# An attention, soft-MoE and MLP kernel: the first pair of heads in an order of its own, its stacks written in place

## The chip, the cores and the metric

The kernel runs on one core of one Trainium2 chip. The metric is device time in microseconds (us) of one execution. Engines are named as in the profile: PE is TensorE (PEld its weight loads), DVE is VectorE, ACT is ScalarE, POOL is GpSimd, SP is SyncE, whose queue issues nearly all DMAs.

## What is computed

Three layers follow one another, all in fp32.

```python
# attention: B = 4, H = 8, S = 576, D = 64
q_rot, k_rot = rotate(q), rotate(k)              # x1*cos - x2*sin, x1*sin + x2*cos
scores = q_rot @ k_rot.T / sqrt(D)
attn = exp(scores - max(scores)); attn /= sum(attn) + 1e-9
x = (attn @ v)                                   # heads side by side: 2304 rows of 512
# soft MoE: 8 experts, 4 slots each, hidden size 1024
logits = x @ phi
slot_in = softmax(logits, over rows).T @ x
slot_out[e] = relu(slot_in[e] @ w1[e]) @ w2[e]
x = softmax(logits, over slots) @ slot_out
# MLP, hidden size 2048
h = x @ w_in
out = (h * tanh(softplus(h))) @ w_out
```

## The kernel before

**Stages.** Attention takes the 32 heads in 16 pairs (0 to 325 us), the experts follow, and then the MLP (from 375 us to the end). While attention runs, other engines already convert the weights of the MLP into pairs of words and load expert weights into buffers that come free.

**Scores.** A head has 576 rows: 512 main rows, in four blocks of 128, and 64 rest rows. Both operands of the score product are split into a high and a low part (fp32r, a form of fp32 that PE takes faster). For each pair they lie in two *stacks*: `qk_st` holds the scaled q of both heads (columns QA and QAR for head 0, QB and QBR for head 1) and the k of both heads (from KC); `k2_st` holds k a second time with the halves exchanged. The high part lies on 64 of the 128 partitions and the low part on the other 64, so that one matmul against `qk_st` and one against `k2_st` make up the product (`s_mm`, L328 ff.). A score step takes 4 matmuls of 128x288, or 8 for the rest rows (`s_mm2`).

**One pair** goes through these steps, each a short name in the order table:
- `ropek`, `ropeq`, `ropeR`: rotation of k, q and the rest rows (`rotate`, L239: two products, a difference and a sum)
- `Hk`, `Hq`, `G`: four PE transposes of k or q (`m_k`, `m_q`), and one of the rest rows (`m_rem`)
- `hka`, `hqa`, `ga`: ACT writes the high part from PSUM into the tile `parth`; `hkd`, `hqd`, `gd`: DVE writes the low part into `partl`
- `dk`, `dq`: 8 and 4 DMAs from SBUF to SBUF that put the parts into the stacks (`stack_dma`, L320)
- S0 to S8: score steps, M0 to M8: row maxima on DVE (`nmax`), E0 to E8: exponentials on ACT (`P`); the even ones belong to head 0, the odd ones to head 1, 8 is the rest rows of both
- T0 to T7, K, R, Q: transposes of the exponentials, t0 to t7, k, ...: their copies from PSUM into `PT` (which engine copies is in `EVAC`, L38)
- A0 to A4 and B0 to B4: the product with v; X, x, Y, y, z, w: scaling of its output and its product with phi
- `ci`, `Ca`, `Cb`, `Cs`, `co`: load, scaling on ACT (`w<-w`), rounding on DVE, sum on POOL and store of a block of MLP weights; `turns` (L719) says which block falls to which pair
- `ld`: loads of q and k for a later pair, and of rest rows for a later batch

**Order.** The order of work on each engine is written out by hand. `PLAN` (L28) is the list of steps of one period, and "@1" after a step means that it is done for the pair before. The loop at the end of attention goes through the periods and records each step in turn. So an instruction that waits holds up all that stands behind it on its engine. All recorded instructions have one line, L83.

**The first pair** has no pair ahead of it that would build its stacks. The setup (L663 ff.) does it: DVE ropes k, the rest rows and q; PE transposes them; ACT and DVE write the parts; `stack_copy` on ACT and POOL moves them into the stacks (seven copies), and one `stack_dma` (two DMAs) moves the low part of head 1's k. In between, `busy` puts idle matmuls on PE. In period 0 the steps that feed pair 1 are moved to later places (`moved`, `shifted`).

**PSUM.** The score buffers `s` are two tiles of two banks (`ps_s`), and four tiles of one bank (`ps_m`) serve all else.

**Weights.** `fetch` (L131) loads a block of expert weights into a buffer of the rings. At `LAST_SCRATCH`, when the scratch of the conversions is free, three blocks are fetched one after the other.

Of the kernel before, what the change touches and what calls it, by code (L numbers as in the profile page):

```python
# [41 lines left out]
def kernel(  # L42
# [185 lines left out]
    def load_rem(b):  # L228
        t = work(1, 3, (H, D))
        dma(out=t[0:R], in_=q[b, :, 512:S, :].rearrange("h s d -> s h d"))  # L230
        dma(out=t[R:128], in_=k[b, :, 512:S, :].rearrange("h s d -> s h d"))
        rem_raw[b] = t
# [473 lines left out]
    main_hi(-1, "q")  # L706
    stack_copy(act.copy, "q", 0, "h")
    main_lo(-1, "q")
    stack_copy(pool_.tensor_copy, "q", 0, "l")
    stack_copy(act.copy, "q", 1, "h")  # L710
    stack_copy(act.copy, "q", 1, "l")
    load_v(1)
# [100 lines left out]
    moved = {(-1, n) for n in ("G", "ga", "gd", "Hk")}  # L813
    moved |= {(0, n) for n in ("hka", "hkd", "dk", "Hq", "hqa", "hqd", "dq", "ropek", "ropeq")}
    steps["ropeq1"] = lambda p: rope_pair(1, "q", dve, ws[1])
    moved |= {(-1, "ld")}
# [436 lines left out]
```

## Time and profile before

| | |
|---|---|
| time, median of 3 runs | 607.31 us (606.13 to 609.28) |
| profiled execution, own time | 609.64 us |
| profiled execution, span | 607.9 us |
| mean granted clock of PE | 0.997 |
| PE busy | 588.2 us, 97% of the span |
| DVE, ACT, POOL busy | 384.1, 341.5 and 213.9 us |
| DMA | 108.82 MB, mean 179 GB/s |

The runs are timed without a profile; the rows further down come from the one profiled execution, whose time is 2.33 us above the median. Its span is 1.74 us shorter than its time. A granted clock of 1.00 is 2.4 GHz, one of 0.50 is 1.2 GHz. Matmuls are pipelined, so that the durations of neighbours overlap.

### The profile page before, as it was taken

How to read it: one execution, taken by the hardware profiler on the slowest of the kernel's cores; microseconds unless marked ns; L12 is line 12 of the kernel's file. 1: busy time of each engine (PE TensorE's matmuls, PEld its weight loads, DVE VectorE, ACT ScalarE, POOL GpSimd, SP SyncE). 2: the span in 40 equal slices, each digit the busy share in tenths (PEclk: the TensorE clock that was granted, in tenths of full speed). 3: DMA queues.
4: the chain of work that ended last, by engine and by line, in shares of the span. 5: the costliest groups of instructions: out<-in, count | busy, mean ns of one | idle time of the engine just before them, and what ended most of it. 6: DMA issues, size and time to landing. Idle time of an engine off the chain costs nothing.

```text
span 607.9 us, 11291 instructions
## 1 busy us (share of the span) xinstructions
PE 588.2 (97%) x4110; PEld 467.0 (77%) x4110; DVE 384.1 (63%) x808; ACT 341.5 (56%) x778; POOL 213.9 (35%) x258
## 2 busy tenths in 40 slices
...
GB/s 173 233 260 213 208 229 267 252 230 263 262 254 260 256 255 275 228 167 312 245 214 379 196 380 402 173 88 156 11 20 85 0 1 1 66 38 0 2 1 105
DMA packets 59288, 108.82 MB, mean 179 GB/s; under 512 B 12768, under 2 KB 25184, under 8 KB 58720
## 3 DMA queue, kind: packets, MB, share of 16 engines
...
## 4 chain that ended last, share of the span: by engine, by line
PE 80%; DMA 6%; DVE 3%; ACT 2%; issue 1%; SPq 0%; ACTq 0%; DVEq 0%
PE o_ps L1137 32%; PE s L83 12%; PE m_av L83 10%; PE t L83 7%; DMA qk_st<-parth 4%; PE hp L1103 3%; PE h_ps L933 2%; PE so_ps L999 2%; PE m_lg L83 2%; PE warm L557 2%; DMA qk_st<-partl 1%; PE m_x L83 1%; PE m_q L83 1%; ACT P L83 1%; PE m_si L83 1%; PE tk L83 1%
## 5 line engine op out<-in xcount | busy, mean ns | idle before, releaser
L83 DVE TENSOR_REDUCE nmax<-s 128x1 f32<-128x576 f32 x144 | 106.8, 751 | 27.1 <-PE s L83 25.6
L83 ACT ACTIVATE P<-s,nmax 128x576 f32<-128x576 f32 x144 | 107.1, 744 | 18.3 <-DVE nmax L83 17.4
L1137 PE MATMUL o_ps<-wo_l,gh 128*128 128x512 f32 x288 | 112.9, 392 | 0.0
L1137 PE MATMUL o_ps<-wo_h,gh 128*128 128x512 f32 x288 | 112.9, 392 | 0.0
L83 PE MATMUL s<-qk_st 128*128 128x288 f32 x320 | 102.5, 337 | 5.3 <-ACT P L83 4.9
L1110 ACT ACTIVATE room<-hp 128x512 f32<-128x512 f32 x72 | 43.0, 599 | 106.6 <-PE hp L1103 102.0
L1137 PE MATMUL o_ps<-wo_h,gl 128*128 128x512 f32 x288 | 100.6, 390 | 1.0 <-DVE gl L1118 1.0
L83 PE MATMUL s<-k_st,qk_st 128*128 128x288 f32 x320 | 89.2, 295 | 0.0
L83 POOL TENSOR_TENSOR w<-w,cs 128x512 f32<-128x512 f32 (+2 forms) x74 | 86.5, 1190 | 0.9
L83 PE MATMUL t<-cs,P 128*128 128x128 f32 x576 | 83.9, 273 | 0.4 <-ACT P L83 0.4
L83 PEld LDWEIGHTS s<-qk_st 128*128 128x128 f32 x320 | 60.2, 188 | 21.5 <-ACT P L83 9.7
L83 POOL TENSOR_TENSOR w<-w 128x256 f32<-128x256 f32 (+2 forms) x86 | 65.7, 785 | 17.4 <-ACT P L83 14.8
L1112 DVE CAST gh<-room 128x512 fp32r<-128x512 f32 x49 | 20.9, 427 | 79.4 <-ACT room L1110 79.2
L83 PEld LDWEIGHTS t<-cs,P 128*128 128x128 f32 x576 | 68.2, 142 | 0.9 <-ACT P L83 0.7
L83 ACT COPY PT<-t 128x512 f32<-128x512 f32 (+1 forms) x112 | 61.3, 558 | 10.4 <-PE t L83 9.6
L1137 PEld LDWEIGHTS o_ps<-wo_h,gl 128*128 128x128 f32 x288 | 53.9, 188 | 13.3 <-DVE gl L1118 1.7
L1137 PEld LDWEIGHTS o_ps<-wo_h,gh 128*128 128x128 f32 x288 | 54.1, 188 | 9.3
L1137 PEld LDWEIGHTS o_ps<-wo_l,gh 128*128 128x128 f32 x288 | 54.3, 189 | 8.9 <-DVE wo_l L990 0.2
L83 PEld LDWEIGHTS s<-k_st,qk_st 128*128 128x128 f32 x320 | 60.6, 189 | 0.0
L1118 DVE TENSOR_TENSOR gl<-room,gh 128x512 fp32r<-128x512 f32 x72 | 49.6, 690 | 4.6
L83 PE MATMUL m_av<-PT,w 128*64 128x320 f32 (+1 forms) x384 | 52.0, 411 | 0.0
L83 POOL TENSOR_TENSOR c_all<-c_all,tmp 128x64 f32<-128x64 f32 (+1 forms) x44 | 20.9, 474 | 57.6 <-DVE tmp L83 55.8
...
## 6 DMA issues: line engine op xcount, KB each, us to landing
...
w<-in_moe_w_in_dram SPq DMA_DIRECT2D x16, 512.0 KB, 5.4
...
room<-in_moe_w_out_dram SPq DMA_DIRECT2D x12, 512.0 KB, 3.5
...
```

What stands on the lines that cost most here:

```text
L83: return lambda *a, **k: tc.keep_in_program_order(f(*a, **k))
L557: tc.keep_in_program_order(nc.tensor.matmul(ps, lhsT=ident, rhs=ident, start=True, stop=True))
L933: nc.tensor.matmul(h_ps[32 * g:32 * g + 32, fh, :], lhsT=si_t[:, c, 32 * e:32 * e + 32], rhs=parts[1, e, hf][0][:, cc * F1 + fh * 512:cc * ...
L999: nc.tensor.matmul(so_ps[32 * g:32 * g + 32, :], lhsT=h_t[eg][:, c, 32 * g:32 * g + 32], rhs=parts[2, e, hf][0][:, cc * DM:(cc + 1) * DM], ...
L1103: pin(nc.tensor.matmul(hp[:, x, :], lhsT=wst[:, f * 128:(f + 1) * 128], rhs=ct[:, i * 256:(i + 1) * 256], start=True, stop=True))
L1110: pin(nc.scalar.activation(out=gg, in_=hp, func=AF.Mish))
L1112: pin((nc.scalar.copy if 0 < u < NG * GR else nc.vector.tensor_copy)(gh, gg))
L1118: pin(nc.vector.tensor_tensor(out=gl, in0=gg, in1=gh.bitcast(F32), op=ALU.subtract))
L1137: pin(nc.tensor.matmul(ops[i, n], lhsT=g_[:, cols], rhs=w_[f], start=(j == 0 and (x, k) == (0, 0)), stop=(j == NG - 1 and all(y[0] != n fo ...
```

## The change

- **PSUM in pair 0.** There are three score buffers and two small ones at first. Two of the score buffers are `xk` and `xq`, which take the transposed k and q of pair 0. After `PLAN0` the pools are closed, and the old ones (two and four) are opened.
- **Setup.** The load of k is issued on ACT's queue, and ACT's table load after it. The rest rows of heads 0 and 1 are loaded alone, behind q; those of the other six heads come after the loads of pair 1. k and q are transposed once. ACT writes eleven high parts from PSUM straight into their places in the stacks, DVE eleven low parts. `parth`, `partl`, the seven copies and the two stack DMAs aren't used for pair 0. The first two score steps stand between the parts. There are 10 and 8 idle matmuls instead of 14, 9 and 12 in the setup, and none in pair 0.
- **POOL** now ropes q of pair 1 too, which DVE did (`ropeq1`).
- **Order of pair 0.** `PLAN0`, a list of its own, takes the place of `moved` and `shifted`. t1 and t3 of pair 0 are copied by DVE. The steps `G`, `ga`, `gd` and `Hk` that feed pair 2 come early in period 1 (`late_feed`). The loads `ld:1`, `ld:2` and the conversion load `ci1` stand at the end of `PLAN0`.
- **Conversions.** The first one moves from pair 0 to pair 1; there are 20 as before.
- **Weight fetch.** At `LAST_SCRATCH` two blocks are fetched instead of three; the third is fetched behind `dk` of pair 14, which holds the stack DMAs of pair 15's k.

The order of the instructions shows it on PE first, from the start of the program (`busy` is idle matmuls, `m_k`, `m_rem` and `m_q` are the transposes, `s` the scores). Before:

```order
L83 MATMUL busy<-c_all 128x128 x14
L83 MATMUL m_k<-cs,w_7_0_96 128x128 x4
L83 MATMUL m_rem<-cs,w_5_1_98 128x128
L83 MATMUL busy<-c_all 128x128 x9
L83 MATMUL m_q<-cs,w_7_0_96 128x128 x4
L83 MATMUL busy<-c_all 128x128 x12
L83 MATMUL s<-qk_st_119 128x288
L83 MATMUL s<-k_st_117,qk_st_119 128x288
```


With the change:

```order
L90 MATMUL busy<-c_all 128x128 x10
L90 MATMUL xk<-cs,w_0_0_85 128x128 x4
L90 MATMUL xk<-cs,w_5_1_98 128x64
L90 MATMUL xq<-cs,w_5_1_98 128x64
L90 MATMUL busy<-c_all 128x128 x8
L90 MATMUL xq<-cs,w_0_0_85 128x128 x4
L90 MATMUL s<-qk_st_119 128x288
L90 MATMUL s<-k_st_117,qk_st_119 128x288
```


The scores follow the transposes of q with no idle matmuls between, and the transposes go into `xk` and `xq`.

On ACT, in pair 0, from its first exponentials on (`P` is an exponential, `parth` a high part for pair 1, `PT` a copy out of PSUM, `w<-w` the scaling of weight words). Before:

```order
L83 ACTIVATE P,z_121<-s,nmax 128x576 x4
L83 CAST parth<-m_rem 128x2x2x64
L83 ACTIVATE parth<-m_k 128x512
L83 ACTIVATE w_4_0_93<-w_4_0_93 128x512 x2
L83 COPY PT<-t 128x4x128 x2
L83 ACTIVATE P,z_121<-s,nmax 128x576
L83 COPY PT<-t 128x4x128
L83 ACTIVATE parth<-m_q 128x512
L83 ACTIVATE P,z_121<-s,nmax 128x576
L83 COPY PT<-t 128x4x128
L83 COPY PT<-tk 128x256
L83 COPY PT<-t 128x4x128
```


With the change:

```order
L90 ACTIVATE P,z_121<-s,nmax 128x576
L90 ACTIVATE parth<-m_k 128x512
L90 ACTIVATE P,z_121<-s,nmax 128x576 x2
L90 COPY PT<-t 128x4x128
L90 ACTIVATE P,z_121<-s,nmax 128x576
L90 CAST parth<-m_rem 128x2x2x64
L90 ACTIVATE P,z_121<-s,nmax 128x576
L90 COPY PT<-t 128x4x128
L90 ACTIVATE P,z_121<-s,nmax 128x576
L90 ACTIVATE parth<-m_q 128x512
L90 ACTIVATE P,z_121<-s,nmax 128x576
L90 COPY PT<-tk 128x256
```


The scaling of weight words is gone from this stretch, the parts for pair 1 are spread between the exponentials, and of the first copies into `PT` fewer stand here.

On SP's queue, from the last stack DMAs of pair 1 on (`w<-in_q`, `w<-in_k` are loads of q and k, those with 8x64 the rest rows; `w<-in_moe_w_in` is a load for a conversion). Before:

```order
L83 DMA qk_st_120<-parth 64x576
L83 DMA qk_st_120<-partl 64x576
L83 DMA w_4_0_93<-in_moe_w_in_dram 128x1024
L83 DMA w_6_0_95<-in_q_dram 128x2x256
L83 DMA w_6_0_95<-in_k_dram 128x2x256
L83 DMA w_5_0_94<-in_q_dram 64x8x64
L83 DMA w_5_0_94<-in_k_dram 64x8x64
L83 DMA w_4_0_93<-in_moe_w_in_dram 128x1024
```


With the change:

```order
L90 DMA qk_st_120<-parth 64x576
L90 DMA qk_st_120<-partl 64x576
L90 DMA w_6_0_95<-in_q_dram 128x2x256
L90 DMA w_6_0_95<-in_k_dram 128x2x256
L90 DMA w_6_0_95<-in_q_dram 128x2x256
L90 DMA w_6_0_95<-in_k_dram 128x2x256
L90 DMA w_5_0_94<-in_q_dram 64x8x64
L90 DMA w_5_0_94<-in_k_dram 64x8x64
L90 DMA w_4_0_93<-in_moe_w_in_dram 128x1024 x2
```


A conversion load stood directly behind the stack DMAs; now six loads stand between.

The diff, cut to its core:

```diff
@@ the order of pair 0, ahead of EVAC @@
+PLAN0 = (
+    "S4 M2 E0 Hk hka E2 M4 S1 E4 T0 M1 hkd S3 t0 E1 G ga gd dk T2 M3 S6 E3 t2 M6 Hq T1 E6 S5 hqa t1 M5 "
+    "hqd dq T3 E5 S7 t3 M7 K0 ld:1 ropek:1 k0 E7 S8 M8 A0 E8 z0 ropeR:1 A1 A2 A3 A4 T4 ropeq:1 x0 t4 T5 "
+    "ld:2 ci1 Y0 y0 t5"
 ).split()
@@ pools @@
-    ps_s = psx.enter_context(tc.tile_pool(name="ps_s", bufs=2, space=PSUM))
-    ps_m = psx.enter_context(tc.tile_pool(name="ps_m", bufs=4, space=PSUM))
+    ps_s = psx.enter_context(tc.tile_pool(name="ps_s0", bufs=3, space=PSUM))
+    ps_m = psx.enter_context(tc.tile_pool(name="ps_m0", bufs=2, space=PSUM))
@@ def t_copy @@
-        out_of(EVAC[f"t{i}"], pt_of(p, t // 2)[:, 5 * h:5 * h + 4, tt * 128:(tt + 1) * 128], m_ps.pop(("T", p, i)))
+        out_of("d" if p == 0 and i in (1, 3) else EVAC[f"t{i}"], pt_of(p, t // 2)[:, 5 * h:5 * h + 4, tt * 128:(tt + 1) * 128], m_ps.pop(("T", p, i)))
@@ setup @@
-    nc.scalar.preload_act_table_set("exp_and_friends")
     pool_.memset(c_all, 0.0)
     dma(out=cs[:, C_COS:C_END], in_=cst[:, C_COS:C_END])
-    load_pair(0, "k")
+    load_pair(0, "k", act.dma_start)
     dma(out=cs[:, 0:C_COS], in_=cst[:, 0:C_COS])
-    load_rem(0)
     load_pair(0, "q")
+    load_rem(0, 0, 2)
+    nc.scalar.preload_act_table_set("exp_and_friends")
...
     load_pair(1, "kq")
+    load_rem(0, 2, H)
...
+    xk, xq = (ps_s.tile([128, 2, 512], F32, tag="s", name="x" + n) for n in "kq")
...
+    first("k", kt, ws[0])
     rope_rem(0, dve, 0, 2)
-    rope_pair(0, "q", dve, ws[1])
-    busy(14)
-    main_pe(-1, "k")
-    rem_pe(-1)
-    busy(9)
-    main_pe(-1, "q")
-    busy(12)
-    parts_of_pair(0)
-    main_hi(-1, "k")
-    rem_hi(-1)
-    stack_copy(act.copy, "k", 0, "h")
-    stack_copy(act.copy, "k", 1, "h")
-    rem_lo(-1)
-    main_lo(-1, "k")
-    stack_copy(pool_.tensor_copy, "k", 0, "l")
-    stack_dma(0, "k", 1, "l")
...
+    first("q", qt, ws[1])
+    busy(10)
+    for c in range(4):
+        pe.transpose(xk[:, c * 128:(c + 1) * 128], kt[:, c, :], ident)
+    pe.transpose(xk[:, 512:S], rem[0][R:128, 0:128], ident[R:128, R:128])
+    pe.transpose(xq[:, 512:S], rem[0][0:R, 0:128], ident[0:R, 0:R])
+    busy(8)
+    for c in range(4):
+        pe.transpose(xq[:, c * 128:(c + 1) * 128], qt[:, c, :], ident)
...
+    hi(ka[up], xk[up, 0:S])
+    hi(k2a[dn], xk[up, 0:S])
+    hi(k2b[dn], xk[dn, 0:S])
+    hi(kb[up], xk[dn, 0:S])
+    hi(qa[up, 0:128], xq[up, 0:128], SCALE)
+    hi(qa[up, 128:512], xq[up, 128:512], SCALE)
+    lo(k2a[up], xk[up, 0:S], ka[up])
+    lo(ka[dn], xk[up, 0:S], ka[up])
+    lo(qa[dn, 0:128], xq[up, 0:128], qa[up, 0:128], SCALE)
+    scores(0, 0)
+    lo(qa[dn, 128:512], xq[up, 128:512], qa[up, 128:512], SCALE)
...
+    maxima(0, 0)
+    lo(kb[dn], xk[dn, 0:S], k2b[dn])
+    lo(k2b[up], xk[dn, 0:S], k2b[dn])
...
+    scores(0, 2)
+    lo(qb[up, 0:512], xq[dn, 0:512], qb[dn, 0:512], SCALE)
...
     rope_pair(1, "k", pool_)
     rope_rem(0, pool_, 2, 4)
+    rope_pair(1, "q", pool_)
...
-    turns = [(p, k) for p in range(NP) for k in range(2) if not k or p % 2 == 0][:NFB * KDM + NCE]
+    turns = [(p, k) for p in range(NP) for k in range(2) if (k if not p else not k or p % 2 == 0 or p == 1)][:NFB * KDM + NCE]
@@ def after @@
-            for i in (0, 0, 2):
-                fetch(ahead.pop(i))
+            for _ in range(2):
+                fetch(ahead.pop(0))
+        if (name, p) == ("dk", NP - 2):
+            fetch(ahead.pop(2))
@@ the loop over the periods @@
-    shifted = {(0, "M3"): [("ropeq1", 0), ("ld", 1)],
-               (0, "S4"): [(n, 0) for n in ("G", "ga", "gd", "Hk", "hka", "hkd", "dk")] + [("ropek", 1)],
-               (0, "S6"): [(n, 0) for n in ("Hq", "hqa", "hqd", "dq")] + [("ropeq", 1)]}
-    for period in range(first, NP + last):
+    begin = [((w + ":0").split(":")[0], int((w + ":0").split(":")[1])) for w in PLAN0]
+    late_feed = [(n, 1) for n in ("G", "ga", "gd", "Hk")]
+    for name, p in begin:
+        steps[name](p)
+    psx.close()
+    ps_s = psx.enter_context(tc.tile_pool(name="ps_s", bufs=2, space=PSUM, reuse_waits="tile"))
+    ps_m = psx.enter_context(tc.tile_pool(name="ps_m", bufs=4, space=PSUM, reuse_waits="tile"))
+    for period in range(1, NP + last):
         for name, n in plan:
             p = period - n
-            if period == 0 and p < 0 and name[0] in "TRKB":
-                busy(1)
-            if 0 <= p < NP and (period, name) not in moved:
+            if (period, name) == (1, "ropek"):
+                for f, i in late_feed:
+                    steps[f](i)
+            if 0 <= p < NP and (name, p) not in begin:
                 steps[name](p)
                 after(name, p)
...
```

## Rows read from the trace of the kernel before

**Rows 1.** Page: busy time of each engine; shares of the chain that ended last.

```profile
PE 588.2 (97%) x4110; PEld 467.0 (77%) x4110; DVE 384.1 (63%) x808; ACT 341.5 (56%) x778; POOL 213.9 (35%) x258
...
PE 80%; DMA 6%; DVE 3%; ACT 2%; issue 1%; SPq 0%; ACTq 0%; DVEq 0%
```

**Rows 2.** Windows: length, busy PE, PEld, DVE, ACT, POOL (instructions), granted clock, DMA, GB/s.

```profile
14.51:33.48 18.97, 16.01 (x122) 13.72 (x123) 13.99 (x22) 12.90 (x30) 18.24 (x21) 1.00 0.88 230
33.48:52.25 18.77, 18.35 (x148) 15.13 (x147) 16.90 (x35) 15.45 (x38) 14.40 (x16) 1.00 0.91 244
52.25:70.22 17.97, 17.97 (x149) 15.10 (x147) 14.10 (x31) 14.39 (x36) 14.11 (x18) 1.00 0.86 224
280.00:300.00 20.00, 20.00 (x166) 15.93 (x166) 13.51 (x30) 13.08 (x33) 1.42 (x4) 1.00 0.87 247
```

**Rows 3.** Timeline of PE, 14 to 34: start, us, instruction, count, idle before.

```profile
14.51 0.40 PE L83 MATMUL s<-qk_st 128*128 128x288 f32 x1 [0.26 <-POOL qk_st L83]
...
28.83 1.95 PE L83 MATMUL m_av<-PT,v 128*64 128x256 f32 x16
...
31.14 0.40 PE L83 MATMUL s<-qk_st 128*128 128x288 f32 x1
...
32.29 0.60 PE L83 MATMUL t<-cs,P 128*128 128x128 f32 x4
...
33.12 0.61 PE L83 MATMUL m_k<-cs,w 128*128 128x128 f32 x4
```

**Rows 4.** Timeline of DVE, 4 to 12.

```profile
4.48 1.29 DVE L83 TENSOR_TENSOR w<-w,cs 128x512 f32<-128x512 f32 x2 [2.12 <-DMA w<-in_k_dram]
...
7.84 0.49 DVE L83 TENSOR_TENSOR w<-w,cs 128x128 f32<-128x128 f32 x2 [1.27 <-DMA w<-in_k_dram]
...
8.65 0.68 DVE L83 TENSOR_TENSOR cvw<-w,cs 128x512 f32<-128x512 f32 x1
...
9.97 0.76 DVE L83 TENSOR_TENSOR w<-w,cvw 128x256 f32<-128x256 f32 x2
...
10.98 0.68 DVE L83 SCALAR_TENSOR_TENSOR partl<-m_k,parth 128x512 fp32r<-128x512 f32 x1
```

**Rows 5.** Timeline of DVE, 19 to 23: pair 1's q rope, beside POOL.

```profile
19.30 0.76 DVE L83 TENSOR_TENSOR cvw<-w,cs 128x512 f32<-128x512 f32 x1
...
20.82 1.30 DVE L83 TENSOR_TENSOR w<-w,cvw 128x256 f32<-128x256 f32 x2
```

**Rows 6.** Timeline of ACT, 12 to 40.

```profile
12.40 0.60 ACT L83 ACTIVATE parth<-m_q 128x512 fp32r<-128x512 f32 x1
...
16.90 0.74 ACT L83 ACTIVATE P<-s,nmax 128x576 f32<-128x576 f32 x1
...
37.90 1.25 ACT L83 ACTIVATE w<-w 128x512 f32<-128x512 f32 x2
```

**Rows 7.** Groups of DVE by form, 0 to 40: count, busy us, mean ns.

```profile
L83 DVE TENSOR_REDUCE nmax<-s 128x1 f32<-128x576 f32 x13 | 9.6, 749 | 2.6 <-PE s L83 2.6
```

**Rows 8.** Timeline of SP's queue, at 30 and at 274.

```profile
30.26 0.59 SPq L83 DMA_DIRECT2D w<-in_moe_w_in_dram  x1
...
274.09 8.53 SPq L147 DMA_DIRECT2D w<-in_moe_w_dram  x3
```

**Rows 9.** DMA issues, 0 to 45: count, KB each, median us to landing.

```profile
w<-in_moe_w_in_dram SPq DMA_DIRECT2D x3, 512.0 KB, 6.3
```

**Rows 10.** Timeline of POOL, 14 to 19.

```profile
14.54 2.52 POOL L83 TENSOR_TENSOR w<-w,cs 128x512 f32<-128x512 f32 x2
17.13 1.43 POOL L83 TENSOR_TENSOR w<-w 128x256 f32<-128x256 f32 x2
```

**Rows 11.** Windows, columns as in the second group.

```profile
24.00:28.00 4.00, 2.01 (x16) 1.72 (x15) 3.93 (x5) 3.16 (x9) 3.92 (x4) 1.00 0.95 222
...
324.00:328.00 4.00, 2.40 (x17) 1.84 (x18) 2.34 (x7) 0.41 (x1) 0.00 (x0) 0.97 1.05 408
328.00:331.00 3.00, 3.00 (x16) 2.78 (x15) 0.71 (x5) 1.25 (x5) 0.00 (x0) 0.50 1.04 353
```

More of the change, by code (lines that the diff above doesn't have):

```diff
@@ L209, with load_pair @@
     xg = {}
-    def load_pair(p, which="qk"):
+    def load_pair(p, which="qk", dma=dma):
         b, h = divmod(2 * p, H)
@@ L226, in load_v, with load_rem @@
         vt[p] = t
[L228 to L232, printed above, removed]
+    def load_rem(b, h0=0, h1=H):
+        t = rem_raw[b] = work(1, 3, (H, D))
+        dma(out=t[0:R, h0:h1], in_=q[b, h0:h1, 512:S, :].rearrange("h s d -> s h d"))
+        dma(out=t[R:128, h0:h1], in_=k[b, h0:h1, 512:S, :].rearrange("h s d -> s h d"))
     def load_vrem(b):
@@ L301, in main_part @@
     def main_part(p, nm, x):
+        if (x, p + 1) not in part:
+            parts_of_pair(p + 1)
         return part[x, p + 1][:, "qk".index(nm), R:R + 512]
@@ L677 @@
     load_pair(1, "kq")
+    load_rem(0, 2, H)
     load_vrem(0)
     load_v(0)
+    st, s2 = qk_st[0], k2_st[0]
+    up, dn = slice(0, 64), slice(64, 128)
+    xk, xq = (ps_s.tile([128, 2, 512], F32, tag="s", name="x" + n) for n in "kq")
+    own = parts[ahead[0]][0]
+    qt, kt = (own[:, o:o + 512].rearrange("p (c x) -> p c x", c=4) for o in (0, 512))
+    none = ps_m.tile([128, 128], F32, tag="m", name="busy")
     def busy(n):
-        ps = ps_m.tile([128, 128], F32, tag="m", name="busy")
         z = c_all[:, 0, 0:4].rearrange("p t s -> p (t s)")
@@ L705, with first @@
-    stack_dma(0, "k", 1, "l")
[L706 to L712, printed above, removed]
+            pe.matmul(none, lhsT=z, rhs=z, start=True, stop=True)
+    def first(nm, t, tb):
+        rotate(raw.pop((nm, 0)), bc(cs[:, C_COS:C_COS + 256], 2), bc(cs[:, C_SIN:C_SIN + 256], 2),
+               t.rearrange("p c (h d) -> p h c d", h=2), 2, 256, dve, tb)
@@ new lines, in hi, with lo @@
+    def hi(out, ps, scale=1.0):
+        act.activation(out=out, in_=ps, func=AF.Copy, scale=scale)
+    def lo(out, ps, hi, scale=1.0):
+        dve.scalar_tensor_tensor(out=out, in0=ps, scalar=scale, in1=hi.bitcast(F32), op0=ALU.mult, op1=ALU.subtract)
+    first("k", kt, ws[0])
+    rope_rem(0, dve, 0, 2)
+    first("q", qt, ws[1])
+    xk, xq = (x.rearrange("p a n -> p (a n)") for x in (xk, xq))
+    busy(10)
+    for c in range(4):
+        pe.transpose(xk[:, c * 128:(c + 1) * 128], kt[:, c, :], ident)
@@ new lines @@
+    hi(k2b[dn], xk[dn, 0:S])
[7 more added lines that the diff above has]
+    lo(qa[dn, 128:512], xq[up, 128:512], qa[up, 128:512], SCALE)
+    hi(qb[dn, 0:512], xq[dn, 0:512], SCALE)
+    hi(k2f[dn], xk[dn, 512:S])
+    hi(kf[up], xk[dn, 512:S])
+    hi(qb[dn, 512:S], xq[dn, 512:S])
```

19 lines of the change are left out of this document (11 added, 8 removed).

## The prediction

> **What bounds the kernel now.** I read the page first: TensorE (PE) is busy for 97% of the span, and the chain that ended last runs through PE for 80% of its length [rows 1]. So the end moves with PE's work, and with the few places where PE waits. The busy time by stretch says where these lie. I cut it at the first score matmul of pairs 0, 1, 2 and 3: pair 0 took 18.97 us with PE busy for 16.01, pair 1 took 18.77 with 18.35, pair 2 took 17.97 with 17.97, and the end of attention (280 to 300) is full [rows 2]. What can be won at the start is therefore the time ahead of the first score, 14.51 us [rows 3], and the waits of pair 0. From pair 2 on PE is never free, so a microsecond won or lost ahead of it is kept to the end. A measurement of this kernel tells about 0.5% (3.04 us) from no change.
>
> The profiled execution took 609.64 us, 2.33 above the median of the runs (607.31). I make the sum against it and take the difference over to the median.
>
> **Step 1, the front: about 2.5 us earlier.** Before, DVE ropes k from 4.48, waits 1.27 for the rest rows of all heads, and ropes them from 7.84 to 8.65 [rows 4]. Now the rest rows of two heads come alone, behind q. I take the wait to be gone: k's rope ends at 6.57 (7.84 less 1.27); issuing k on ACT's queue moves this by 0.1 at most, since DVE was waiting for data then. The rest follows by 7.35. Then q's rope: alone it took 2.08 (8.65 to 9.97 + 0.76) [rows 4], beside a working POOL 2.82 (19.30 to 20.82 + 1.30) [rows 5]. POOL starts the rope of pair 1's k now, so I take 2.5, between the two: 9.85.
>
> Meanwhile PE transposes k and the rest (ready at 7.75), and ACT writes four high parts, each 0.60 like its other reads of a PSUM tile [rows 6]: 10.2. DVE's first low part begins there, not at 9.85, because the code's order makes DVE's reads of `xk` follow ACT's. Two low parts of 0.69, as DVE's 0.68 for the same operation [rows 4], end at 11.6. ACT has the first 128 columns of q ready by then, a short low part of 0.25 follows (estimated from the 128-column pair, 0.49 for two [rows 4]), and the first score starts at 11.9 to 12.1, against 14.51: **2.5 earlier**. Bounds: 11.2 (q's rope undisturbed, the low parts not held by ACT) and 13.0 (rope at 2.82, half of the old 1.27 wait still there).
>
> What is removed, seven copies into the stacks on ACT and POOL and two stack DMAs, was on that path: the old first score waited for POOL's copy [rows 3].
>
> **Step 2, pair 0 in its own order: 0.1 more.** In the new order PE is rarely the bound; ACT and DVE hand over to each other. I go through it op by op: maxima (M) 0.75 [rows 7], an exponential (E) 0.74 [rows 6], high part or copy 0.60, low part or DVE copy 0.69 at a pitch of 0.61, four transposes 0.5, and 0.1 at each hand-over.
> - Score at 12.0, M0 done at 13.6, four low parts of k and three of q behind it until 16.1, M2 until 16.8.
> - ACT: E2, E4, t0, E1 and `ga` until 20.1; DVE: `gd` and M3 until 21.2; E3 until 22.1; t2 until 22.7.
> - With two small PSUM buffers T1 has to wait for t2: T1, t1, M5, `hqd`, T3, t3 in a row, 0.5 + 0.69 + 0.75 + 0.61 + 0.5 + 0.69 = 3.7 and hand-overs: 26.7.
> - The five A blocks, 2.31 (28.83 to 31.14), then T4, T5 and Y0. One T and one Y0 took 0.83 (32.29 to 33.12) [rows 3], with T5 1.3: 30.3, and 30.5 with hand-overs. I take 30.7.
>
> Pair 1 begins at 30.7 instead of 33.48: 2.8 earlier. Four transposes take about 0.4 (33.12 to 33.48, `m_k`) [rows 2, 3]. T5 is now already done (0.4), but `G` and `Hk` of pair 2, five transposes, now stand behind pair 1's first score (0.5), so **2.7** is what is won in all by then. The waits in this order are as long as the old ones: 18.7 from score to score, against 18.97. That the stall goes from the stacks to the two buffers is why so little is added. Bounds: 1.5 (front at 13.0) and 3.5 (front at 11.2).
>
> **Step 3, the first weight conversion comes late: 1.4 lost.** Before, the second conversion load was issued at 30.26, and ACT scaled its words at 37.90 [rows 6, 8]. Now SP first takes twelve stack DMAs. The eight of k can't start before `ga` (20.1) and the four of q, 0.59 each by the load in the same queue, not before `hqd` (25.3): 27.7. Then it takes six loads for pairs 3 and 4, which also wait for POOL's ropes to leave their buffers, 0.59 each at most, 3.4 in all: 31.1. Only then come the two conversion loads. Landing takes 6.3 [rows 9]: 37.4. ACT wants the words 4.42 after pair 1's first score (37.90 less 33.48), which is 35.1, and I add 0.5 for the feed of pair 2 now ahead of them: 35.6. ACT waits 1.8 with PSUM copies queued behind it that PE needs. PE idled 0.42 in that pair already [rows 2], so PE loses **1.4**. Bounds: 0 (512 KB alone at the 230 GB/s of this stretch [rows 2] take 2.2) and 4.3 (the second load of 512 KB is served together with the first, 2.2 more, and some of the slack is gone).
>
> **Step 4, edits at nothing.** The third weight block goes behind the stack DMAs of pair 15's k. The three fetches held SP for 8.53 from 274.09, with the stacks of the next pair's k behind them [rows 8]; two hold it for a third less, 2.8. But PE is busy for all of 280 to 300 [rows 2], so nothing waited. Without that cover it would be worth up to 0.4, or cost as much if the third block came late. The conversions moved from pair 0 to pair 1 are as many as before and run beside a full PE. The moved q rope of pair 1 leaves DVE, 2.82, and lengthens POOL's row of ropes, which delivers it ahead of `Hq`. Fewer fillers ahead of the first transposes: 0.2 lost to transposes at the lower clock, bounds 0 and 1.
>
> **Sum.** 609.64 - 2.7 + 1.4 + 0.2 = 608.5 for a profiled execution, 1.1 less than before. At the median: 607.31 - 1.1 = **606.2**. That is within 0.5%, so no change that can be told.
>
> **Rivals.**
> *Faster: the conversion isn't late and the front meets its early bound.* For it: loads of this stretch run beside others, and 2.2 would do for 512 KB. Against it: six loads and twelve stacks are ahead on one queue. Gain 3.5, less 0.1 for the clock: 603.9.
>
> *Slower: DVE and POOL block each other in the front.* DVE's q rope of pair 0 (four operations, each with two inputs in SBUF) now runs beside POOL's k rope of pair 1. If every one of the four had to wait for one POOL operation to end, the wait would be 2 x 1.26 + 2 x 0.72 = 3.96 [rows 10], where my sum has 0.4 (2.5 against 2.08): 3.5 later, 607.31 - 1.1 + 3.5 = 609.7, 2.4 slower than before. It decides as soon as more than two of the four wait a full operation. Against it: the same rope beside POOL took only 2.82, 0.74 longer than alone [rows 4, 5]. The Trainium skill ("SBUF — State Buffer", Who interferes with whom) says that a DVE operation with two SBUF inputs and a GpSimd operation that reads SBUF share a port by an exclusive lock, and that the loser blocks for the whole instruction; by it the time would be this rival's. The measured 0.74 speaks for a milder form, so it has 0.1. With the late conversion at its upper bound as well it would be near 612.
>
> *The clock falls in the thinned front.* Between the transposes of q and the second group of scores PE now has little to do. Before, the granted clock was 0.50 in 328 to 331, after a stretch where PE was busy for 2.40 of 4 us; yet 24 to 28, with 2.01 of 4, kept 1.00 [rows 11]. If it falls for 3 us of matmuls, about 1 is lost: 607.3. The Trainium skill ("TensorE: Matmul & The Clock Gate", What's actually happening) says that throttled is the default and that activity releases it; by that rule the thinner front is at risk, and of the two rows here one agrees and one doesn't.
>
> *The late load at its upper bound* (4.3 less 0.4 instead of 1.4): 608.7.
>
> **How the numbers follow.** Forecast 0.45, the faster rival 0.17, the clock 0.20, the port 0.10, the late load 0.08. All but parts of the first two and combinations of the last three stay within 3.04 of 607.31. Faster needs a time under 604.27: nearly the whole faster rival, 0.15. Slower needs over 610.35: the port together with a late load or a lower clock, 0.12. Between them 0.73. The range goes from the faster rival with 0.3 for the spread of the runs (603.6) to the port rival (609.6).
>
> **What would show it.** First score of pair 0 at 11.9 to 12.1; pair 1's at 30.6 to 30.9; DVE's q rope 2.3 to 2.8 long; T1 and T3 behind t2 and `hqd`; ACT idle before its scaling of words in pair 1, released by a DMA, and PE idle there for 1 to 2; no PE wait in 280 to 300; after that the same work, 1 earlier. I am wrong if the first score comes after 13, if pair 1 has no wait for the conversion, or if a clock of 0.50 shows up before 40 us.

## The result, and the profile after

| | before | changed |
|---|---|---|
| time, median of 4 runs each | 606.83 us (606.13 to 609.28) | 615.81 us (615.06 to 617.97) |
| profiled execution: time, span | 609.64, 607.9 | 615.24, 613.5 |
| mean granted clock | 0.997 | 0.986 |
| first score of pair 0, 1, 2 | 14.51, 33.48, 52.25 | 14.05, 34.22, 58.55 |

A fourth run of the kernel before brings its median from 607.31 to 606.83. The changed kernel is slower: ratio 1.0147, 95% interval 1.0107 to 1.0186, about 9 us. The forecast was 606.2 with a range of 603.6 to 609.6, so it missed, and to the wrong side. The two traces differ by 5.6 us of span only, since the profiled execution of before was itself 2.8 above its median.

The page of the changed kernel, the same two lines as [rows 1]:

```profile
PE 587.8 (96%) x4059; PEld 465.0 (76%) x4059; DVE 387.8 (63%) x814; ACT 339.1 (55%) x777; POOL 216.7 (35%) x259
...
PE 63%; DMA 5%; DVE 2%; ACT 1%; POOL 1%; issue 0%; SPq 0%; DVEq 0%; ACTq 0%
```

PE does the same amount of work, so the loss is waiting or a lower clock. The windows, cut at the first scores as in [rows 2] (length, busy PE, PEld, DVE, ACT, POOL, granted clock, DMA share, GB/s), show where:

```profile
14.05:34.22 20.17, 16.27 (x99) 13.42 (x100) 12.86 (x24) 11.96 (x31) 14.56 (x18) 0.83 0.48 114
34.22:58.55 24.33, 20.65 (x153) 16.94 (x152) 16.88 (x35) 15.45 (x37) 13.09 (x14) 0.93 0.86 225
58.55:76.53 17.98, 17.98 (x148) 15.10 (x147) 15.83 (x34) 15.42 (x38) 16.86 (x20) 1.00 0.86 227
280.00:300.00 20.00, 20.00 (x166) 15.80 (x165) 13.90 (x32) 13.45 (x36) 5.76 (x9) 1.00 0.92 297
8.00:12.00 4.00, 3.28 (x18) 2.98 (x16) 3.96 (x4) 2.58 (x4) 3.92 (x4) 0.57 0.79 184
16.00:22.00 6.00, 5.32 (x22) 5.21 (x23) 5.11 (x11) 2.66 (x8) 5.67 (x6) 0.50 0.00 0
31.50:43.60 12.10, 10.39 (x80) 7.69 (x76) 5.95 (x12) 5.03 (x13) 4.24 (x5) 1.00 0.99 246
41.80:45.60 3.80, 0.20 (x2) 0.00 (x0) 1.21 (x3) 1.92 (x5) 0.00 (x0) 1.00 1.06 222
45.00:50.00 5.00, 4.39 (x21) 3.72 (x22) 3.40 (x9) 4.19 (x11) 2.34 (x2) 0.66 0.91 217
```

Pair 0 took 20.17 instead of 18.97, and pair 1 took 24.33 instead of 18.77. In pair 2 (17.98 and 17.97) and in 280 to 300 the two kernels are alike. So these two traces put the loss into the first 59 us: 6.3 us at pair 2's first score. The rest of the 9 us is not located. The clock was at 0.50 for most of 8 to 12 (mean 0.57) and for all of 16 to 22, and lower again in 45 to 50, right behind the long wait of pair 1.

That wait, on PE, on ACT and on SP's queue (start, us, instruction, idle time before and its releaser):

```profile
45.61 0.87 PE L90 MATMUL m_av<-PT,w 128*64 128x320 f32 x4 [3.61 <-ACT PT L90]
```

```profile
43.64 1.21 ACT L90 ACTIVATE w<-w 128x512 f32<-128x512 f32 x2 [4.56 <-DMA w<-in_moe_w_in_dram]
44.74 0.59 ACT L90 ACTIVATE parth<-m_q 128x512 fp32r<-128x512 f32 x1
45.35 0.20 ACT L90 COPY PT<-t4r 64x64 f32<-64x64 f32 x1
```

```profile
23.50 0.53 SPq L90 DMA_DIRECT2D qk_st<-parth  x1
...
31.50 0.54 SPq L90 DMA_DIRECT2D w<-in_q_dram  x1
...
35.07 1.09 SPq L90 DMA_DIRECT2D w<-in_moe_w_in_dram  x2
```

The two conversion loads were issued at 35.07, behind twelve stack DMAs from 23.50 and six loads from 31.50. ACT waited 4.56 for the first of them, with the high part of q and a copy (`PT<-t4r`) queued behind, and PE waited 3.61 for that copy. The table of DMA issues gives 9.4 us to landing for these two, against 6.3 in [rows 9]:

```profile
w<-in_moe_w_in_dram SPq DMA_DIRECT2D x2, 512.0 KB, 9.4
```

The front, on DVE and POOL:

```profile
4.85 1.30 DVE L90 TENSOR_TENSOR w<-w,cs 128x512 f32<-128x512 f32 x2 [2.48 <-DMA w<-in_k_dram]
...
6.86 0.49 DVE L90 TENSOR_TENSOR w<-w,cs 128x128 f32<-128x128 f32 x2
...
7.66 0.68 DVE L90 TENSOR_TENSOR cvw<-w,cs 128x512 f32<-128x512 f32 x1
8.26 1.76 DVE L90 TENSOR_TENSOR w<-w,cs 128x512 f32<-128x512 f32 x1
10.05 2.23 DVE L90 TENSOR_TENSOR w<-w,cvw 128x256 f32<-128x256 f32 x2
12.21 0.74 DVE L90 SCALAR_TENSOR_TENSOR k_st<-xk,qk_st 64x576 fp32r<-64x576 f32 x1
12.96 0.75 DVE L90 SCALAR_TENSOR_TENSOR qk_st<-xk,qk_st 64x576 fp32r<-64x576 f32 x1
```

```profile
7.82 3.32 POOL L90 TENSOR_TENSOR w<-w,cs 128x512 f32<-128x512 f32 x2 [6.21 <-DVE w L90]
```

The rest rows are no longer waited for (6.86 follows k's rope). But q's rope runs from 7.66 to 12.28, 4.62 us, against 2.08 in [rows 4], and POOL's products beside it take 3.32 instead of 2.52 [rows 10]. The low parts come one every 0.75.

### The profile page after: what moved, and what is told of

Read it like the earlier page. It is cut to its first block, busy times and chain, and to the rows that moved or that the text cites. A ratio compares the mean times of both kernels' runs of the same rounds, so it can differ in the third digit from the quotient of the medians.

```text
span 613.5 us, 11190 instructions
## 1 busy us (share of the span) xinstructions
PE 587.8 (96%) x4059; PEld 465.0 (76%) x4059; DVE 387.8 (63%) x814; ACT 339.1 (55%) x777; POOL 216.7 (35%) x259
## 4 chain that ended last, share of the span: by engine, by line
PE 63%; DMA 5%; DVE 2%; ACT 1%; POOL 1%; issue 0%; SPq 0%; DVEq 0%; ACTq 0%
PE o_ps L1182 32%; PE s L90 6%; PE m_av L90 6%; PE t L90 4%; DMA qk_st<-partl 3%; PE hp L1148 3%; PE h_ps L978 2%; PE so_ps L1044 2%; PE warm L565 2%; DMA qk_st<-parth 1%; PE m_lg L90 1%; PE m_wp L1125 1%; DMA w<-in_q_dram 1%; PE m_ct L941 1%; PE m_x L90 1%; PE m_si L90 1%
## 5 line engine op out<-in xcount | busy, mean ns | idle before, releaser
L90 ACT ACTIVATE P<-s,nmax 128x576 f32<-128x576 f32 x144 | 107.2, 746 | 20.0 <-DVE nmax L90 18.7
L90 PE MATMUL s<-qk_st 128*128 128x288 f32 x320 | 104.1, 341 | 4.7 <-ACT P L90 2.9
L90 POOL TENSOR_TENSOR w<-w,cs 128x512 f32<-128x512 f32 (+2 forms) x76 | 89.7, 1202 | 13.5 <-DMA w<-in_k_dram 6.4
L90 PE MATMUL s<-k_st,qk_st 128*128 128x288 f32 x320 | 90.7, 299 | 0.0
L90 PE MATMUL t<-cs,P 128*128 128x128 f32 x576 | 85.7, 276 | 2.0 <-ACT PT L90 1.3
L90 PEld LDWEIGHTS s<-qk_st 128*128 128x128 f32 x320 | 61.5, 192 | 19.5 <-issue 8.2
L90 POOL TENSOR_TENSOR w<-w 128x256 f32<-128x256 f32 (+2 forms) x88 | 67.5, 788 | 18.8 <-ACT P L90 9.7
L90 ACT COPY PT<-t 128x512 f32<-128x512 f32 (+1 forms) x110 | 60.5, 559 | 11.3 <-PE t L90 10.2
L90 PEld LDWEIGHTS s<-k_st,qk_st 128*128 128x128 f32 x320 | 62.0, 194 | 0.0
L90 PEld LDWEIGHTS m_av<-PT,w 128*64 128x64 f32 x384 | 25.7, 136 | 22.3 <-ACT PT L90 5.5
```

The lines of the kernel that those rows point to most:

```text
L90: return lambda *a, **k: tc.keep_in_program_order(f(*a, **k))
```

## The experiments

Three causes stood out: the conversion load, DVE against POOL, and the clock. The rival was that the new order of pair 0 with two small PSUM buffers is what costs. Of each run I read the first scores of pairs 0, 1 and 2 from PE's timeline, because whole executions of one kernel spread by some 8 us (605 to 613 for before). Each row is one profiled execution. The three that have before's front (before, w1, b1) put the first score within 0.8 of each other (13.72 to 14.51), and their pair 0 within 0.02. "Pair 0" and "pair 1" are the differences. Ratios are to runs of the kernel before, taken beside those of the run.

| run | first scores | pair 0 | pair 1 | ratio (95%) |
|---|---|---|---|---|
| before | 14.51, 33.48, 52.25 | 18.97 | 18.77 | 1 |
| changed | 14.05, 34.22, 58.55 | 20.17 | 24.33 | 1.0147 (1.0107 to 1.0186) |
| e1 conversion early | 14.07, 34.77, 53.66 | 20.70 | 18.89 | 1.0033 (1.0003 to 1.0064) |
| e2 POOL after q | 12.88, 33.04, 57.97 | 20.16 | 24.93 | 1.0063 (1.0021 to 1.0106) |
| e3 idle matmuls | 15.08, 34.79, 59.72 | 19.71 | 24.93 | 1.0130 (1.0082 to 1.0178) |
| e4 all three | 15.14, 34.84, 53.74 | 19.70 | 18.90 | 1.0041 (1.0008 to 1.0075) |
| w1 before, fetch moved | 13.72, 32.67, 51.35 | 18.95 | 18.68 | 1.0008 (0.9974 to 1.0042) |
| b1 before, conversion late | 13.85, 32.80, 51.85 | 18.95 | 19.05 | 0.9996 (0.9968 to 1.0024) |
| e5 = e1 + e2 | 12.74, 32.20, 51.08 | 19.46 | 18.88 | 0.9995 (0.9959 to 1.0032) |
| e6 = e5 + few idle matmuls | 12.16, 31.37, 50.23 | 19.21 | 18.86 | 1.0009 (0.9982 to 1.0036) |
| e10 = e6 + M3 ahead | 13.28, 32.08, 50.94 | 18.80 | 18.86 | 0.9994 (0.9966 to 1.0021) |
| e13 = e6 + new list | 12.59, 30.42, 49.71 | 17.83 | 19.29 | 0.9960 (0.9932 to 0.9989) |

**e1: the conversion loads early.**

```diff
 PLAN0 = (
-    "S4 M2 E0 Hk hka E2 M4 S1 E4 T0 M1 hkd S3 t0 E1 G ga gd dk T2 M3 S6 E3 t2 M6 Hq T1 E6 S5 hqa t1 M5 "
+    "ci1 ci0:1 S4 M2 E0 Hk hka E2 M4 S1 E4 T0 M1 hkd S3 t0 E1 G ga gd dk T2 M3 S6 E3 t2 M6 Hq T1 E6 S5 hqa t1 M5 "
...
-    "ld:2 ci1 Y0 y0 t5"
+    "ld:2 Y0 y0 t5"
```

> The changed kernel with one edit: its first two conversion loads are issued on SP's queue ahead of the stack DMAs of pair 1, in the stretch where the DMA engines stand idle (11 to 23 us), instead of behind the loads of pairs 3 and 4. Theory (the late conversion load is the largest part of the loss): ACT's wait of 4.56 us and PE's of 3.61 in pair 1 go, and so does the half clock right after them; pair 1 takes about 18.8 us instead of 24.33, the time falls by 5.0 to 5.6 us, from 615.8 to about 610.5. Rival (the two small PSUM buffers and the new order of pair 0 are what costs, and pair 1 waits for whatever comes next, the stacks of pair 2): 2 us or less, 614 or more.

Measured: pair 1 takes 18.89 instead of 24.33, 5.44 less, at a clock of 1.00 throughout. On SP's queue the two loads go at 11.63, ahead of the stack DMAs, and ACT scales without a wait:

```profile
34.77:53.66 18.89, 18.81 (x152) 15.61 (x152) 16.71 (x35) 15.28 (x37) 13.10 (x14) 1.00 0.91 235
```

```profile
11.63 0.94 SPq L90 DMA_DIRECT2D w<-in_moe_w_in_dram  x2
```

```profile
39.52 1.26 ACT L90 ACTIVATE w<-w 128x512 f32<-128x512 f32 x2
```

The ratio falls from 1.0147 to 1.0033. The theory holds: the place of these two loads is most of the loss. Of the 5.44, PE's wait is 3.61; the rest is the lower clock behind it, since PE is busy for 20.65 in the slow pair and for 18.81 in this one with the same work. At pair 2 only 4.89 of it is left, because pair 0 was 0.53 longer here (20.70), at a mean clock of 0.79 instead of 0.83.

**e2: POOL behind DVE's rope of q.**

```diff
-    first("q", qt, ws[1])
+    first("q", qt, None)
```

With no scratch given, q's rope takes the one that POOL's rope needs next.

> The changed kernel with one edit: DVE's rope of q of pair 0 uses the scratch that POOL's first rope uses too, so POOL starts only when DVE is done. Theory (DVE and POOL block each other in the front): q's rope takes 2.1 us instead of 4.62, the first score starts at about 11.6 instead of 14.05, and the time falls by 2 to 2.5 us, unless the clock falls earlier for it; from 615.8 to about 613.5. Rival (pair 0 is bound by its hand-overs between ACT and DVE and by its two small buffers, so that an earlier front is lost again in pair 0): the first score is earlier as well, but pair 1 starts less than 0.5 earlier. Rival (the four operations are slow for another reason than POOL): the rope stays at 4 us or more.

DVE's rope of q takes 2.09 (7.48 to 9.57) with POOL standing:

```profile
7.48 1.30 DVE L90 TENSOR_TENSOR w<-w,cs 128x512 f32<-128x512 f32 x2
8.81 0.76 DVE L90 TENSOR_TENSOR w<-w,w 128x256 f32<-128x256 f32 x2
10.46 0.75 DVE L90 SCALAR_TENSOR_TENSOR k_st<-xk,qk_st 64x576 fp32r<-64x576 f32 x1 [0.88 <-ACT qk_st L90]
```

```profile
9.65 2.50 POOL L90 TENSOR_TENSOR w<-w,cs 128x512 f32<-128x512 f32 x2 [8.04 <-DVE w L90]
```

```profile
7.71 3.68 PE L90 MATMUL busy<-c_all 128*128 128x128 f32 x16
11.23 0.60 PE L90 MATMUL xq<-cs,w 128*128 128x128 f32 x4
```

So POOL made it 2.53 longer. The first score comes at 12.88, 1.17 earlier and not at 11.6: the low parts now wait for ACT's four high parts (the 0.88), and the idle matmuls ahead of q's transposes, at a clock of 0.50, held these until 11.23, though the rope had ended at 9.57. All of the 1.17 reaches pair 1. Pair 1 still has its wait, and pair 2 starts only 0.58 earlier. The median, 613.68, is where the theory put it, but the trace doesn't carry that; the ratio fell by about 5 us, and its wide interval doesn't let me weigh it. The Trainium skill ("SBUF — State Buffer", Who interferes with whom) has a DVE operation with two inputs in SBUF contend with a GpSimd one that reads SBUF, and this agrees in kind: both engines were longer together. With the full price of 3.96 q's rope would have taken 6.0.

**e3: idle matmuls on PE, and e4: all three.**

```diff
-    busy(8)
+    busy(16)
...
         pe.transpose(xq[:, c * 128:(c + 1) * 128], qt[:, c, :], ident)
+    busy(8)
...
     scores(0, 0)
+    busy(14)
```

> The changed kernel with one edit: idle matmuls put back on PE, 16 instead of 8 ahead of the transposes of q, 8 ahead of the first score and 14 behind it. Theory (the thinned front lets the clock fall, and pair 0 pays for it): the granted clock stays at 1.00 from 8 to 30 us, where it was 0.50 in 16 to 22; pair 0 is 2 to 2.7 us shorter, and the time goes from 615.8 to about 613.5. Rival (PE isn't what bounds pair 0, ACT and DVE are): the clock stays up, but pair 1 starts less than 0.5 us earlier.

> The three edits of the other runs of this call at once: conversion loads early, POOL's rope behind DVE's, idle matmuls. Theory (three separate causes that add up): 5.3 + 2.3 + 2.3, 10 us less than the changed kernel, 605.9, about 1 under the kernel before. First score near 11.6, pair 1's at about 30.5, pair 2's at about 49.3, clock 1.00 throughout. Rival (the parts hide one another, or something else in pair 0 takes their place): 608 or more.

The clock was 1.00 in 16 to 22, with 5.56 of 6 us busy:

```profile
16.00:22.00 6.00, 5.56 (x48) 5.33 (x46) 5.88 (x12) 2.74 (x8) 5.08 (x6) 1.00 0.00 0
```

Both missed their times, and the rival of each holds: pair 1's first score came at 34.79 and 34.84, against 34.22. There were too many: they stood ahead of q's transposes and of the first score, which came at 15.08 and 15.14. From first to first score, pair 0 was only 0.46 shorter in e3 (19.71 against 20.17). That is less than the half clock costs, because the 14 behind the first score are in the way themselves: they hold the second group of scores until 18.74, 3.66 behind the first score, where it was 2.63 in the changed kernel. e6 below is the better measure.

**w1: the weight fetch alone, on the kernel before.**

```diff
-            for i in (0, 0, 2):
-                fetch(ahead.pop(i))
+            for _ in range(2):
+                fetch(ahead.pop(0))
+        if (name, p) == ("dk", NP - 2):
+            fetch(ahead.pop(2))
```

> The kernel before with one part of the change: two blocks of expert weights fetched at the old place, the third behind the stack DMAs of pair 15's k. Theory (PE is full there, so the fetch's place is worth nothing): within 1 us of the kernel before, PE busy for all of 280 to 300. Rival (the late third block or the earlier stacks count): 1 us or more, either way.

Ratio 1.0008, and PE is busy for all of 280 to 300: nothing, within the 0.4% of the interval. What this run also shows is the front of before in another execution:

```profile
6.14 0.76 DVE L83 TENSOR_TENSOR w<-w,w 128x256 f32<-128x256 f32 x2
7.01 0.49 DVE L83 TENSOR_TENSOR w<-w,cs 128x128 f32<-128x128 f32 x2
```

Here the rest rows were waited for by 0.1 to 0.2 only, and the first score came at 13.72. In b1, with the same front, the wait was 0.63 and the score at 13.85. The 1.27 of [rows 4] was this one execution's.

**b1: a late conversion load alone, on the kernel before.**

```diff
-    moved |= {(-1, "ld")}
+    moved |= {(-1, "ld"), (0, "ci1")}
...
+               (0, "Y0"): [("ci1", 0)],
```

> The kernel before with one part of the change: its second conversion load goes behind the loads of pair 3 and of the rest rows (four loads, not six as in the changed kernel), directly ahead of the next conversion load. Theory (the place of this load alone makes pair 1 long): it is issued 2 to 3 us later, at about 33, lands at 40 to 42, ACT waits 2 to 4 us ahead of its scaling of words, PE loses 1 to 3 in pair 1, and pair 2 starts at 53.5 to 55.5 instead of 52.25; the time is 1 to 4 us above before. Rival (it hurts only with the rest of the change, six loads and the feed of pair 2 ahead of it): pair 1 below 19.0 us.

```profile
32.69 1.92 SPq L83 DMA_DIRECT2D w<-in_moe_w_in_dram  x2
```

```profile
38.18 1.27 ACT L83 ACTIVATE w<-w 128x512 f32<-128x512 f32 x2 [1.06 <-DMA w<-in_moe_w_in_dram]
```

A miss: ACT waited 1.06, not 2 to 4, pair 1 took 19.05, and the ratio is 0.9996. The rival's 19.0 is met but for 0.05. The place behind four loads alone costs about 0.3. Counted from pair 1's first score, ACT wanted the words at much the same time in both (4.3 here, 4.9 in the changed kernel), and the issue differs by 1 us (0.1 ahead of it here, 0.85 behind it there). The larger difference is the landing: 5.5 from issue to ACT here, 8.6 there, where two more loads were ahead. In the changed kernel the DMA engines had no room then (share 0.99 from 31.50 to 43.60). What made the landing longer was not tried alone.

**e5: e1 and e2 together.**

> The changed kernel with two edits: conversion loads early and POOL's first rope behind DVE's rope of q; no idle matmuls added. Theory (conversion 5.4 us, and of the contention in the front only what reaches pair 1, 1.2): 609 us, 1 to 2 above the kernel before; DVE's rope of q 2.1 us, first score 12.9, pair 1's first at 33.0 to 33.5, a clock of 0.50 twice before 22. Rival (the clock falls longer in the front once it is shorter, and takes the gain back): pair 1 not earlier than in the run with the conversion loads alone (34.8).

Pair 1's first score came at 32.20, 2.57 earlier than in e1 and earlier than the theory's 33.0, and the ratio is 0.9995: with these two repairs the changed kernel is level with before. Of the 2.57, 1.33 is the first score. The other 1.24 is pair 0. POOL's place alone left that as it was (20.16 in e2); what differs from e1 is the clock, which here fell only once before 22, from 17 to 21.

**e6: idle matmuls sized to the waits.** The edit against e5:

```diff
-    busy(8)
+    busy(6)
...
+    busy(9)
...
     scores(0, 0)
+    busy(7)
```

> The same two edits, and idle matmuls sized to the waits of PE as they are without contention: 6 ahead of the transposes of q, 9 ahead of the first score, 7 behind it. In the earlier run with 16, 8 and 14 the idle matmuls themselves stood ahead of q's transposes for 3 us and hid what the clock is worth. Theory (the half clock delays the transposes of pair 1's k and so the exponentials that stand behind their high part on ACT): clock 1.00 from 2 to 30, first score 12.8, pair 1's first at 32.0 to 32.5, about 1 us less than without them: 607 to 608. Rival (pair 0 is bound by ACT and DVE whatever the clock): pair 1's first score within 0.3 of the run without them.

```profile
16.00:22.00 6.00, 4.74 (x33) 3.85 (x33) 4.78 (x10) 3.73 (x10) 5.76 (x7) 1.00 0.40 145
```

The clock held. Pair 1's first score came 0.83 earlier than in e5, at 31.37: outside the rival's 0.3 and near the theory's 1. But only 0.25 of it is in pair 0, where the theory had it; 0.58 is the first score, at 12.16. The time can't be told from e5's.

Now pair 0 can be set beside its clock. The runs up to here have the same list of steps but for the two loads. Without the added idle matmuls of e3 and e4, pair 0 took 19.21 at a mean clock of 1.00 (e6), 19.46 at 0.91 (e5), 20.16 and 20.17 at 0.83 (e2, changed) and 20.70 at 0.79 (e1):

```profile
14.07:34.77 20.70, 16.91 (x99) 13.73 (x100) 12.86 (x24) 12.05 (x31) 14.27 (x17) 0.79 0.62 164
12.74:32.20 19.46, 15.43 (x99) 12.48 (x100) 12.86 (x24) 11.94 (x31) 16.44 (x22) 0.91 0.72 193
12.16:31.37 19.21, 15.84 (x115) 12.55 (x114) 12.75 (x24) 11.94 (x31) 16.95 (x22) 1.00 0.75 208
```

So the half clock goes with about 1 us of the changed kernel's pair 0. No run changed the clock and nothing else, so the cause is argued from this order.

**e10: T2 and M3 ahead of gd.** The edit against e6:

```diff
-    "ci1 ci0:1 S4 M2 E0 Hk hka E2 M4 S1 E4 T0 M1 hkd S3 t0 E1 G ga gd dk T2 M3 S6 E3 t2 M6 Hq T1 E6 S5 hqa t1 M5 "
+    "ci1 ci0:1 S4 M2 E0 Hk hka E2 M4 S1 E4 T0 M1 hkd S3 t0 E1 G ga T2 M3 gd dk S6 E3 t2 M6 Hq T1 E6 S5 hqa t1 M5 "
```

> The run above with one move in the list of pair 0: T2 and M3 stand ahead of gd and dk, so that DVE takes the maxima of score 3 while it would wait for ACT's high part of the rest rows (1.23 us in the changed kernel). Theory (the new order has a chain of its own through gd, M3, E3, t2 and T1, which the two small buffers make): pair 1's first score 1.0 to 1.3 us earlier than without the move, at 31 to 31.5, and the time 1 less, 606.5, level with the kernel before or just under it. Rival (the chain runs through other steps): less than 0.4 earlier.

From the first score to Y0 of pair 0 it takes 17.49 us (13.28 to 30.77), against 18.74 in e6 (12.16 to 30.90): 1.25, the size that the theory had. But pair 1's first score, which was to come 1.0 to 1.3 earlier, came 0.71 later than in e6, at 32.08. One reason is the stacks, for which PE's weight load waited; this leaves pair 0 only 0.41 shorter:

```profile
30.77 0.66 PE L90 MATMUL m_lg<-phi_sb,xts 128*128 128x64 f32 x4
32.08 0.37 PE L90 MATMUL s<-qk_st 128*128 128x288 f32 x1 [0.65 <-issue]
```

```profile
32.05 0.19 PEld L90 LDWEIGHTS s<-qk_st 128*128 128x128 f32 x1 [0.75 <-DMA qk_st<-parth]
```

`gd` came later, the low part of k held the queue for 1.83, and the stack DMAs of head 0's q went at 28.11 and 28.75, to land 3.2 to 3.3 later. The other reason is the first score, 1.12 later than in e6 with the same front. Here PE ran slowly for longer at the start. The rows give a clock of 1.00, but PE, full in both, got through 7 matmuls in 9 to 10 and 11 in 12 to 13:

```profile
9.00:10.00 1.00, 1.00 (x7) 1.00 (x6) 0.73 (x2) 0.99 (x2) 0.18 (x1) 1.00 0.78 245
12.00:13.00 1.00, 1.00 (x11) 1.00 (x10) 1.00 (x3) 0.20 (x1) 0.92 (x2) 1.00 0.99 285
```

The traces' clock records begin only at the first rise, at 4.4 to 10.9 us depending on the execution, and the rows count what lies ahead of it as 1.00. Up to it idle matmuls start every 0.21 us, behind it every 0.11. It came late, at 10.4 to 10.9, in e3, e4, e5 and e10.

**e13: a list in which the stack DMAs go early.** The edit against e6:

```diff
-    "ci1 ci0:1 S4 M2 E0 Hk hka E2 M4 S1 E4 T0 M1 hkd S3 t0 E1 G ga gd dk T2 M3 S6 E3 t2 M6 Hq T1 E6 S5 hqa t1 M5 "
-    "hqd dq T3 E5 S7 t3 M7 K0 ld:1 ropek:1 k0 E7 S8 M8 A0 E8 z0 ropeR:1 A1 A2 A3 A4 T4 ropeq:1 x0 t4 T5 "
-    "ld:2 Y0 y0 t5"
+    "ci1 ci0:1 S4 M2 E0 Hk hka E2 G ga M4 hkd gd dk S1 E4 T0 M1 S3 t0 E1 T2 M3 S6 E3 t2 Hq hqa M6 hqd dq T1 E6 S5 t1 M5 T3 E5 S7 t3 M7 K0 ld:1 ropek:1 k0 E7 S8 M8 A0 E8 z0 ropeR:1 A1 A2 A3 A4 T4 ropeq:1 x0 t4 T5 ld:2 Y0 y0 t5"
```

> The run with early conversion loads, POOL's rope behind q's and sized idle matmuls, and a new list for pair 0: G, ga, gd and dk ahead of S1, T2 and M3 ahead of S6, hqa and hqd ahead of T1, so that the stack DMAs of pair 1 are issued earlier than in the run with M3 ahead, which waited for them. Theory (after M3 the stack DMAs are what holds pair 1): pair 1's first score at 30.5 to 31.3 with no wait of PE there, pair 2's at 49.0 to 50.0, 2.3 to 3.2 earlier than before; the time 2 us under before, 606. Rival (the small PSUM buffers make m_rem and T0 wait for each other, and it moves the stall ahead): pair 1's first score at 31.5 or later.

```profile
29.95 0.66 PE L88 MATMUL m_lg<-phi_sb,xts 128*128 128x64 f32 x4
30.42 0.38 PE L88 MATMUL s<-qk_st 128*128 128x288 f32 x1
```

Pair 1 starts at 30.42 with no wait, pair 2 at 49.71, and the ratio is 0.9960 (0.9932 to 0.9989): median 606.61 against 608.85. This version is 2.2 us under the kernel before, 0.4%, with an interval that leaves 1 out. The trace has as much at pair 2 (49.71 against 51.35 to 52.25). Of the rival from the start of this section, that the new order costs, this much holds: with the three causes repaired (e6) pair 0 still took 19.21, 0.24 more than before, and it is the order that e13 changes to get 17.83.

## Why the prediction was wrong

The forecast had pair 2's first score at about 51.0 (30.7, and 20.3 for pair 1); it came at 58.55. Of the 7.6 between, 2.0 were lost by pair 0's first score, 1.5 in pair 0 and 4.1 in pair 1. Two of the text's three signs of being wrong came: the first score after 13, and a clock of 0.50 before 40.

- **Step 3 is the step that failed most, in size.** Mechanism, place and sign were right (ACT's scaling waits for the load, PE for the copy behind it), but it was put at 1.4 and cost 5.44 (e1). The load was issued at 35.07 and not at 31.1, since the stack DMAs began at 23.50 and not at 20.1: `ga` and `gd` were late with the rest of pair 0. But ACT wanted the words later too, at 39.08 and not at 35.6. Counted from pair 1's first score, the issue was 0.45 later than forecast and ACT's demand was where it had been put. Two terms were too small. The load took 8.6 to reach ACT (35.07 to 43.64), not 6.3, a median of loads with less ahead of them. And the term for the clock behind a wait of PE was missing altogether: 1.83. Even the upper bound, 4.3 for ACT, fell short of 4.56. (Six loads at 0.59 are 3.5 and not the 3.4 of the sum; they took 3.57.)
- **Step 1 failed in size as well: 0.46 instead of 2.5.** "I take 2.5, between the two" for q's rope was the wrong choice: it took 4.62, and POOL is shown as the cause (e2: 2.09). The row of 2.82 that I preferred was of a rope beside other operations of POOL. Without POOL the first score came at 12.74 (e5) and, with fewer idle matmuls ahead of q's transposes, at 12.16 (e6), close to the forecast: the low parts start behind ACT's four high parts, as forecast, at 10.8 and 10.4 instead of 10.2, and take 0.75 each instead of 0.69. And part of what was to be won, the 1.27, wasn't there in other executions of before.
- **Step 2: 1.2 lost instead of 0.1 won.** The chain was the one forecast: in the changed kernel T1 waits 1.28 for t2, and DVE 1.23 for `ga` ahead of M3. The half clock goes with about 1 of the loss (20.17 against 19.21 in e6; argued, see there): at 0.50 ACT waited 3.34 for the transposes of pair 1's k, in e6 2.39. The sum had no term for it; it was priced only among the rivals. The rest, 0.5 of 18.7, includes low parts at 0.76. That `gd` holds M3 was in the chain, and worth 1.25 (e10).

```profile
26.00 0.66 PE L90 MATMUL t<-cs,P 128*128 128x128 f32 x4 [1.28 <-ACT PT L90]
```

```profile
23.51 0.42 DVE L90 TENSOR_TENSOR partl<-m_rem,parth 128x256 fp32r<-128x256 f32 x1 [1.23 <-ACT parth L90]
```

- **Step 4 was right on the fetch:** it is worth nothing (w1), and PE is full in 280 to 300. The conversion moved into pair 1 costs 0.1 to 0.2 when its loads come early (18.89 in e1 against 18.77 and 18.68). The step's 0.2 for the clock was too little.
- **The rivals were right, and the weight of their coming together was too low.** The port rival had 0.10, the clock 0.20, the late load 0.08. The prediction did name a case of two, near 612, and gave all times over 610.35 a chance of 0.12; but its range ended at 609.6, with one rival, and all three came. With all three the text's own prices give 606.2 + 3.5 + 1.1 + 2.5 = 613.3, still under 615.8. That one brought on the others is not shown: without POOL in the way the clock still fell (e2, e5), and pair 1's wait came without POOL (e2) and with the clock held in pair 0 (e3), at 24.93 both times.

What stays open: why the load landed so late; and the ratio of e2, which fell from 1.0147 to 1.0063, while pair 2 starts only 0.58 earlier in its trace. Whether the wait of pair 1 is shorter in other executions was not tried. In the three traces that have it (the changed kernel, e2, e3) pair 1 took 24.33 to 24.93.
